# Second weight of the second MoE: plain blocks in DRAM and a split in place in the steps that load it, with new order keys for that MoE

## The chip, the cores and the metric

The kernel runs on one core of one Trainium2 chip. The metric is the time of one execution in microseconds of device time; the time of a kernel is the median of its runs. One execution is also recorded by the hardware profiler, and the rows below come from that one.

## The reference, cut to what matters

Three stages follow one another in fp32: a packed attention (4 batches, 8 heads, 576 positions), a first feed-forward block with `h * cos(h)` as its activation, and a second one with four experts whose outputs are weighted and summed. The change lies in the last stage alone:

```
N, D, E, F = 2304, 512, 4, 1024
p = domain_probs / (domain_probs.sum(-1, keepdims=True) + 1e-09)
out = zeros(N, D)
for e in range(E):
    h = maximum(x @ w1[e], 0.0)
    out += p[:, e:e + 1] * (h @ w2[e])
```

`w2` is the second weight that the title speaks of.

## The kernel before, in words

**Arithmetic.** TensorE multiplies fp32r operands. Each operand is kept as two tiles, a high part and a low part (the value minus its high part), and `mm3` (line 197) makes three matmuls for one product: high by high (L199), high by low (L200), low by high (L201). Making the two parts is called a split: ScalarE copies the value into the high part (L661), and GpSimd or VectorE subtracts that from the value (L652, the helper `split`).

**Steps of the second MoE.** The 2304 tokens are worked in three thirds (`NH` = 3), and the experts' 4 times 1024 hidden columns in eight slices of 512 (`NU` = 8). One third by one slice is a step, 24 in all, numbered n = 0 to 23. A step has a front, `b_pair` (L901), called twice (j = 0, 1): seven products of a Strassen-like scheme (`PRODUCTS`, L648), each of six matmuls of 384 columns, so 84 in a step. Their sums are made on VectorE (`add`, L931), with one copy on ScalarE for each call (L993). The back of a step stands in the order one step later:

- In the first third (steps 0 to 7) it is `b_back` (L1024): six token tiles, twelve matmuls each of 512 columns, with the four plain row blocks of w2 (tiles `w2`, keys 0 to 3) as moving operand. It ends in L1051 on VectorE.
- In the other two thirds (steps 8 to 23) it is `b_back2` (L1073), again seven products, 84 matmuls of 384 columns. They use the four plain blocks and four sums of w2's quarters, called w1 to w4 there. Its order is `BACK` (L1067): a11, w4, a12, w1, w3, w2, a22. Each ends in L1108 on VectorE. Before it, the gated activations are summed (L960) and split (`g_op`, L965), seven for each call.

**Weights.** In steps 0 to 7 `weights` (L696) loads raw blocks of w1 and w2 (`raw`, four buffers), makes the sums on VectorE (L729, `sums`), and splits seven operands of the front (tag `aop`, eight buffers) and eight of the back (tag `w2`, eight buffers: four blocks, four sums). Although `b_back` reads only the four blocks, the four sums are split too, and all fifteen split tiles, 512 KB each, are written to DRAM by `to_dram` (L670). In steps 8 to 23 `kept_weights` (L677) loads those fifteen tiles, already split, 512 KB each. The back's loads come in the order 0, 1, 2, 3, w1, w3, w2, w4 into a ring of eight buffers, so that each waits until the same buffer's last reader of the step before is done, and none is issued ahead of the one in front of it in the ring. `tokens_kept` (L805) and `kept_tokens` (L869) do for the token operands of the second and third thirds what these two do for the weights; `shares` (L886) loads, every second step, the experts' weights per token.

**Order of the work.** All instructions are put in order by a planner, class `Plan` (L27), before the program is built. Each piece of work has an engine, an assumed duration, what it waits for, the buffers that it takes, and a key. The planner takes whatever can start soonest; among pieces that can start at the same time the lower key goes first. Pieces on engines other than TensorE and the queue of SyncE (SP) take the lowest key of those who wait for them. Work of GpSimd and VectorE work on SBUF alone are never planned at the same time (`port`). A split that has `alt` may go to VectorE. A transfer is planned to occupy SP for its megabytes times `MB2` and to land 2.2 us later; `MB2` is 1/0.4 before. Every engine then runs its list in that order.

The keys of the second MoE's steps are written by hand: step n starts at k0 = 100 times its number, and `PLACE` (L1290) adds offsets:

```
PLACE = ((0, 5, 15, 20, 30, 35, 40), (10, 25, 45), (15, 30, 45, 60, 72, 84, 96))
```

The first tuple is for the seven products of `b_pair` (plus 50 for j = 1), the second for `b_back` and the third for `b_back2`, whose seven offsets belong to `BACK` in its order.

## Time and profile before

| what | value |
|---|---|
| median of 3 runs | 1175.41 us (1173.87 to 1177.24) |
| the profiled execution, its own time | 1176.87 us |
| span of its records, first to last instruction | 1175.1 us |
| TensorE busy | 1106.1 us, 94% of the span |
| VectorE, ScalarE, GpSimd busy | 832.7, 460.0, 453.4 us |
| moved by DMA | 296.23 MB, mean 252 GB/s |

The second MoE begins at about 396 us of the span. A busy TensorE row counts matmuls that overlap one another, so idle time shows only where a matmul waited long; the time between the starts of two matmuls is the better measure of pace.

### The profile page before, as it was taken

To read this page: it belongs to the slowest core of one execution; us is meant where nothing else is said; L and a number is where in the kernel's file an instruction comes from. 1 tells how busy PE (TensorE), PEld (TensorE's weight loads), DVE (VectorE), ACT (ScalarE), POOL (GpSimd) and SP (SyncE) were. 2 spreads that over 40 slices of the span, in tenths; PEclk is the share of its full clock that TensorE was granted. 3 is DMA by queue.
4 is the path that set the end of the run, shared out by engine and by line. 5 is a ranking of instruction groups with operands and counts; after the bars stand their busy time and mean duration, and the time that the engine had idled before them with its cause. 6 is when DMAs were issued, how large, how long until landed. Compare 5 with 4: busy or idle time off the path is not lost.

```text
span 1175.1 us, 19040 instructions
## 1 busy us (share of the span) xinstructions
PE 1106.1 (94%) x7241; PEld 1037.8 (88%) x7241; DVE 832.7 (71%) x1315; ACT 460.0 (39%) x788; POOL 453.4 (39%) x342
## 2 busy tenths in 40 slices
PE   7599999999999989998999999999999999999997
PEld 4478999999999978887878899999999999999997
DVE  3798777865456766678686576777777767767776
ACT  3677655554444434444344233222222232222221
POOL 1454665562224664564554133222222232222220
PEclk7799999999999999999999999999999999999999
DMA  9682433421244797998998998777777997767753
GB/s 312 225 273 95 158 117 148 149 81 41 82 143 147 271 355 281 386 387 334 406 374 324 378 373 304 269 266 270 269 256 287 391 322 262 256 239 267 250 212 125
DMA packets 101646, 296.23 MB, mean 252 GB/s; under 512 B 11500, under 2 KB 32052, under 8 KB 99508
## 3 DMA queue, kind: packets, MB, share of 16 engines
q1 hardware_dynamic: 101556, 295.02, 69.1%
q8 instruction: 57, 0.93, 0.3%
q14 instruction: 33, 0.27, 0.1%
HBM read 206.87 MB, written 88.12 MB: 251 GB/s over the span
## 4 chain that ended last, share of the span: by engine, by line
PE 73%; DMA 11%; DVE 7%; ACT 3%; issue 2%; POOL 2%; SPq 1%; DVEq 0%; ACTq 0%; POOLq 0%
PE pa L199 24%; PE pa L201 23%; PE pa L200 23%; PE pa L347 2%; DMA raw<-w 2%; DMA w<-q0w 1%; DMA w<-q3w 1%; DMA w<-q5w 1%; DVE aop L652 1%; POOL w2s L652 1%; DVE s L729 1%; DMA kt<-kT 1%; DMA w<-q1w 1%; DVE p L931 1%; DMA w<-q6w 1%
## 5 line engine op out<-in xcount | busy, mean ns | idle before, releaser
L199 PE MATMUL pa<-g,w 128*128 128x288 f32 (+1 forms) x960 | 304.8, 317 | 17.3 <-DMA w<-q3w 4.9
L200 PE MATMUL pa<-g,w 128*128 128x288 f32 (+1 forms) x960 | 302.3, 315 | 1.1 <-POOL g L584 1.1
L201 PE MATMUL pa<-g,w 128*128 128x288 f32 (+1 forms) x960 | 302.2, 315 | 0.5 <-POOL w L291 0.5
L652 POOL TENSOR_TENSOR g<-u,g 128x384 fp32r<-128x384 f32 x127 | 132.3, 1056 | 347.3 <-ACT g L661 329.8
L199 PE MATMUL pa<-bop,aop 128*128 128x384 f32 x672 | 229.6, 342 | 17.9 <-DVE p L931 7.6
L201 PE MATMUL pa<-bop,aop 128*128 128x384 f32 x672 | 228.7, 340 | 3.9 <-DVE aop L652 3.1
L200 PE MATMUL pa<-bop,aop 128*128 128x384 f32 x672 | 227.5, 338 | 0.0
L199 PEld LDWEIGHTS pa<-g,w 128*128 128x128 f32 x960 | 180.4, 188 | 24.8 <-issue 10.1
L200 PEld LDWEIGHTS pa<-g,w 128*128 128x128 f32 x960 | 180.5, 188 | 1.8 <-POOL g L584 1.8
L201 PEld LDWEIGHTS pa<-g,w 128*128 128x128 f32 x960 | 180.8, 188 | 1.0 <-POOL w L291 1.0
L661 ACT ACTIVATE g<-u 128x384 fp32r<-128x384 f32 x192 | 98.7, 523 | 191.5 <-DVE u L960 117.8
L199 PEld LDWEIGHTS pa<-bop,aop 128*128 128x128 f32 x672 | 127.5, 190 | 25.5 <-ACT w L661 7.4
L584 POOL TENSOR_TENSOR g<-t,g 128x576 fp32r<-128x576 f32 x64 | 95.2, 1500 | 119.1 <-ACT g L581 113.9
L201 PEld LDWEIGHTS pa<-bop,aop 128*128 128x128 f32 x672 | 127.2, 189 | 5.8 <-DVE aop L652 4.7
L200 PEld LDWEIGHTS pa<-bop,aop 128*128 128x128 f32 x672 | 127.5, 190 | 1.4
L931 DVE TENSOR_TENSOR p<-pa,p 128x384 f32<-128x384 f32 x144 | 79.8, 555 | 45.0 <-PE pa L201 38.8
L1108 DVE TENSOR_TENSOR acc<-pa,acc 128x768 f32<-128x768 f32 x88 | 83.9, 954 | 24.5 <-PE pa L201 24.4
L199 PE MATMUL pa<-at,m 128*128 128x288 f32 x256 | 78.3, 306 | 4.8 <-DVE t L577 3.6
L200 PE MATMUL pa<-at,m 128*128 128x288 f32 x256 | 77.1, 301 | 2.6 <-POOL at L652 2.6
L201 PE MATMUL pa<-at,m 128*128 128x288 f32 x256 | 76.8, 300 | 0.0
L199 PE MATMUL pa<-w,g 128*128 128x512 f32 x192 | 75.2, 392 | 0.0
L201 PE MATMUL pa<-w,g 128*128 128x512 f32 x192 | 75.2, 391 | 0.0
(128 smaller groups left out, 1744.6 us busy)
## 6 DMA issues: line engine op xcount, KB each, us to landing
w<-p SPq DMA_DIRECT2D x64, 512.0 KB, 5.2
at<-at SPq DMA_DIRECT2D x16, 1152.0 KB, 5.3
raw<-w SPq DMA_DIRECT2D x32, 512.0 KB, 6.3
p<-w SPq DMA_DIRECT2D x32, 512.0 KB, 5.9
raw<-w_in SPq DMA_DIRECT2D x6, 1024.0 KB, 5.2
raw<-w_out SPq DMA_DIRECT2D x6, 1024.0 KB, 7.1
vt<-vk SPq DMA_DIRECT2D x8, 576.0 KB, 7.2
kt<-kT SPq DMA_DIRECT2D x8, 576.0 KB, 9.1
```

The costliest lines, as they stand in the source:

```text
L199: nc.tensor.matmul(o, lhsT=l(0), rhs=r(0), start=first, stop=False, skip_group_check=True)
L200: nc.tensor.matmul(o, lhsT=l(0), rhs=r(1), start=False, stop=False, skip_group_check=True)
L201: nc.tensor.matmul(o, lhsT=l(1), rhs=r(0), start=False, stop=last, skip_group_check=True)
L347: nc.tensor.matmul(o(e)[32 * q:32 * q + 32, :N], lhsT=l[64 * e:64 * e + 64, 32 * q:32 * q + 32], rhs=r(q // 2, q % 2)[64 * e:64 * e + 64], ...
L584: nc.gpsimd.tensor_tensor(out=s["g"][:, 1], in0=s["t"], in1=s["g"][:, 0].bitcast(F32), op=ALU.subtract)
L652: (nc.vector if on_vector else nc.gpsimd).tensor_tensor(out=dst[:, 1], in0=src, in1=dst[:, 0].bitcast(F32), op=ALU.subtract)
L661: nc.scalar.activation(r["t"][:, 0], src(), AF.Copy)
L729: nc.vector.tensor_tensor(out=t, in0=src(a, m)(), in1=src(b, m)(), op=o)
L931: nc.vector.tensor_tensor(out=s[o] if o in s else tmp(o), in0=s[x], in1=s[y], op=ALU.add)
L1108: nc.vector.tensor_tensor(out=ac["t"], in0=ac["t"] if how == ALU.subtract else p, in1=p if how == ALU.subtract else ac["t"], op=how)
```

## The change

It does five things.

1. In the first third the four sums of w2 (w1 to w4) are no longer split. The sums themselves go to DRAM as plain fp32, 256 KB each.
2. The four plain blocks of w2 are still split for `b_back`, but what goes to DRAM is the raw block, 256 KB, straight from the tile that was loaded, and not the split pair.
3. In steps 8 to 23 each of the eight w2 tiles is loaded as 256 KB into the low half of its split tile; then ScalarE copies it to the high half, and GpSimd (or VectorE) subtracts in place.
4. The keys of the second MoE come from tables: `first` for n = 0, `one` for steps 1 to 7, `two` for 8 to 22, `end` for 23, `last` for the final back, with entries for stores (`keep`), gated splits (`g`) and the two calls of `tokens_kept` (`kept`, 150 before in both).
5. The planner's figure `MB2` goes from 1/0.4 to 1/0.37.

```diff
-    MB2 = 1 / 0.4
+    MB2 = 1 / 0.37
...
+    def plain(u, x, src, shape, ready, slot, at):
+        def f():
+            w2_d[u, x] = dpool.tile(shape, F32, tag=f"w{u}{x}", name=f"w{u}{x}", bufs=1)
+            nc.sync.dma_start(out=w2_d[u, x], in_=src())
+
+        return dma(0.26 * MB2, f, [ready], [], [slot], at)
...
+        def split_in_place(x, shape, src, after):
+            W[x] = r = {"slot": pl.slot("w2")}
+            at = 100 * len(its) + 100 * n + 50
+
+            def f():
+                r["t"] = bp["w2"].tile(shape, F32R, tag="w2", name="w2", bufs=8)
+                load(r["t"][:, 1].bitcast(F32), src())
+
+            def f_hi():
+                nc.scalar.activation(r["t"][:, 0], r["t"][:, 1].bitcast(F32), AF.Copy)
+
+            def f_lo(v=False):
+                split(r["t"], r["t"][:, 1].bitcast(F32), v)
+
+            a = dma(0.26 * MB2, f, after, [r["slot"]])
+            a = pl.op("ACT", 0.63, f_hi, [a], [], [r["slot"]])
+            r["ready"] = pl.op("POOL", 1.3, f_lo, [a], [], [r["slot"]], alt=0.7)
+
...
-        for x in (0, 1, 2, 3, "w1", "w3", "w2", "w4"):
-            kept(x, "w2", w2_d, [P, 2, 512] if x in range(4) else [P, 2, 2, 256])
+        for k in range(4):
+            split_in_place(k, [P, 2, 512], lambda k=k: w2_d[u, k], [w2_d["op", u, k]])
+        for x in ("w1", "w3", "w2", "w4"):
+            split_in_place(x, [P, 2, 2, 256], lambda x=x: w2_d[u, x], [w2_d["op", u, x]])
...
-        keep = 100 * len(its) + 100 * n + 60
+        keep = 100 * len(its) + 100 * n + KEYS["keep"][0]
...
-            w2_d["op", u, k] = to_dram(w2_d, (u, k), [P, 2, 512], f"p{u}{k}", lambda k=k: W[k]["t"], W[k], keep + 30)
-        sums(2, keep + 40)
+            w2_d["op", u, k] = plain(u, k, lambda k=k: raw[2, k // 2][:, k % 2], [P, 512], ld[2, k // 2], sr[2, k // 2], keep + KEYS["keep"][1])
+        sums(2, keep + KEYS["keep"][2])
         for i in range(1, 5):
-            x = f"w{i}"
-            W[x] = hi_lo("w2", lambda: bp["w2"].tile([P, 2, 2, 256], F32R, tag="w2", name="w2s", bufs=8), src(f"s{i}", 2),
-                         (0.63, 1.3, 0.61), need(2, f"s{i}"), uses(2, f"s{i}"), 3, keep + 50)
-            w2_d["op", u, x] = to_dram(w2_d, (u, x), [P, 2, 2, 256], f"q{u}{x}", lambda x=x: W[x]["t"], W[x], keep + 60)
+            w2_d["op", u, f"w{i}"] = plain(u, f"w{i}", src(f"s{i}", 2), [P, 2, 256], S[2, f"s{i}"]["op"], S[2, f"s{i}"]["slot"],
+                                           keep + KEYS["keep"][3])
...
+        gkey = keys[6] + KEYS["g"][j]
...
-            gkey = k[6] + 40
...
+            'end': {'a': [7.7, -4.1, 13.5, 9.7, 25.5, 36.8, 44.1, 51.4, 31.1, 65.2, 55.6, 83.4, 100, 147.1],
+                    'b': [7.6, 30, 37.1, 56.9, 58.3, 96.2, 118.8]},
...
+            'first': {'a': [-2.9, -27.5, 4.6, 13.1, 46.9, -9.5, 50.4, 5, 11.5, 37, 54.3, 58.5, 40.6, 95.8]},
+            'g': [38.7, 40.8],
...
+            'keep': [100.6, -134.8, 1.6, 6.3],
+            'kept': [169.3, 260.8],
+            'last': {'b': [18.3, 53.6, 64, 91.6, 70.2, 69.5, 211.3]},
...
+            'one': {'a': [27.2, 17, 18.9, 77, 37, 81.6, 28.9, 33.7, 63.9, 48.4, 67, 78.4, 79.5, 60.1],
+                    'b': [25.1, 36, 39.1, 80, 56, 81.7]},
+            'out0': [-122.9, -853.4],
+            'two': {'a': [-6.8, 28.5, 26, 19.7, 29.1, 43.6, 40, 7.4, 46.4, 66, 71.1, 67.6, 82, 91.3],
+                    'b': [15, 25.5, 40.7, 56.3, 70.6, 84.4, 93.8]}}
...
-    PLACE = ((0, 5, 15, 20, 30, 35, 40), (10, 25, 45), (15, 30, 45, 60, 72, 84, 96))
...
+        place = KEYS["first"] if n == 0 else KEYS["one"] if h == 0 else KEYS["end"] if n >= NSTEP - 1 else KEYS["two"]
         if n > NU:
-            b_back2(n - 1, Ws.pop(n - 1), [k0 + x for x in PLACE[2]])
+            b_back2(n - 1, Ws.pop(n - 1), [k0 + x for x in KEYS["last" if n == NSTEP else "two" if n < NSTEP - 1 else "end"]["b"]])
...
-            tokens_kept((n + 1) // 2, k0 + 150)
+            tokens_kept((n + 1) // 2, k0 + KEYS["kept"][n // 2])
```

## Rows read from the trace of the kernel before

**Rows 1.** Page, parts 1 and 2: TensorE's busy time; DMA's busy tenths in 40 slices.
```profile
PE 1106.1 (94%) x7241; PEld 1037.8 (88%) x7241; DVE 832.7 (71%) x1315; ACT 460.0 (39%) x788; POOL 453.4 (39%) x342
...
DMA  9682433421244797998998998777777997767753
```
**Rows 2.** Busy time by stretch; its first line names the columns.
```profile
core 0: us, PE busy (x) PEld busy (x) DVE busy (x) ACT busy (x) POOL busy (x), PEclk, DMA share, GB/s
...
411.80:657.40 245.60, 226.53 (x1095) 199.04 (x1094) 178.70 (x277) 101.88 (x192) 121.77 (x83) 0.99 0.94 358
657.40:1123.50 466.10, 448.16 (x2510) 440.28 (x2509) 340.97 (x570) 127.24 (x247) 126.90 (x122) 1.00 0.80 290
813.50:842.90 29.40, 29.40 (x170) 29.40 (x169) 23.49 (x40) 8.12 (x16) 8.31 (x8) 1.00 0.74 260
...
1123.50:1175.10 51.60, 44.37 (x253) 43.72 (x251) 37.43 (x58) 10.19 (x20) 10.32 (x10) 0.98 0.40 142
```
**Rows 3.** Timeline of TensorE in a back of the first third: start, duration.
```profile
545.17 0.39 PE L200 MATMUL pa<-w,g 128*128 128x512 f32 x1
545.40 0.39 PE L201 MATMUL pa<-w,g 128*128 128x512 f32 x1
```
**Rows 4.** What TensorE waited for, 396 to 657.4 us: total, times, longest.
```profile
PE pa L199 <- DVE p L931: 7.1, 5, 2.5
PE pa L199 <- ACT w L661: 4.4, 3, 2.0
PE pa L201 <- DVE aop L652: 3.1, 5, 1.1
PE pa L199 <- ACT g L980: 2.7, 3, 0.9
PE pa L199 <- ACT p L993: 1.0, 1, 1.0
PE pa L199 <- DVE g L983: 0.8, 1, 0.8
PE pa L201 <- POOL aop L652: 0.7, 1, 0.7
```
**Rows 5.** What TensorE waited for, 657.4 to 1123.5 us.
```profile
PE pa L199 <- DMA w<-q3w: 4.9, 2, 2.5
...
PE pa L199 <- DVE g L652: 4.1, 3, 2.3
...
PE pa L199 <- DMA w<-q4w: 0.5, 1, 0.5
```
**Rows 6.** Timelines of SP's queue and TensorE around the wait at 787 us.
```profile
779.98 0.99 SPq L191 DMA_DIRECT2D w<-q3w  x2
...
789.32 0.41 PE L199 MATMUL pa<-g,w 128*128 128x384 f32 x1 [2.54 <-DMA w<-q3w]
```
**Rows 7.** ScalarE's and GpSimd's groups, 411.8 to 657.4: busy, mean ns, idle before.
```profile
L661 ACT ACTIVATE w<-raw 128x512 fp32r<-128x512 f32 x28 | 17.0, 622 | 20.9 <-DMA q4w<-w2s 5.2 <-DMA q3w<-w2s 5.0 <-DMA q2w<-w2s 3.2
...
L652 POOL TENSOR_TENSOR w2s<-s,w2s 128x512 fp32r<-128x512 f32 x27 | 39.2, 1478 | 68.8 <-ACT w2s L661 68.8
```
**Rows 8.** Transfers by kind: issues, KB each, median us from issue to landing.
```profile
w<-p SPq DMA_DIRECT2D x64, 512.0 KB, 5.2
...
ptile<-pT SPq DMA_DIRECT2D x1, 256.0 KB, 2.9
```
**Rows 9.** VectorE's and ScalarE's groups, 657.4 to 1123.5 us.
```profile
L960 DVE TENSOR_TENSOR u<-u 128x384 f32<-128x384 f32 x58 | 33.5, 578 | 0.9
...
L652 DVE TENSOR_TENSOR g<-p,g 128x384 fp32r<-128x384 f32 x25 | 14.4, 578 | 4.3 <-ACT g L661 2.8
...
L993 ACT ACTIVATE p<-pa 128x384 f32<-128x384 f32 x30 | 14.8, 492 | 74.0 <-PE pa L201 74.0
```
**Rows 10.** Splits of the sums of w2, 411.8 to 657.4: ns min/median/max.
```profile
L652 POOL TENSOR_TENSOR w2s<-s,w2s x27: 1262/1305/2010, 412.3 to 656.0; 128x512 fp32r<-128x512 f32 x27
...
L652 DVE TENSOR_TENSOR w2s<-s,w2s x3: 681/682/844, 452.3 to 657.2; 128x512 fp32r<-128x512 f32 x3
```

## The prediction made before the change was run

> **What bounds the kernel now.** I read the page first: TensorE is busy for 94% of the span, and the DMA engines are nearly full in the middle slices [rows 1]. So TensorE sets the time, and what can be won is where it falls behind its own pace. Then the busy times by stretch. The stretch 813.5 to 842.9 is step 13, with 168 matmuls and no gap: 29.40 us, or 0.175 a matmul of 384 columns [rows 2]. That is the pace of a step in the last two thirds. Matmuls of 512 columns start 0.23 us apart [rows 3], so a step of the first third has a pace of 84 times 0.175 (14.7) plus 72 times 0.23 (16.6), 31.3 us.
>
> Against these paces the rows of stretches say what is lost. Steps 1 to 7 run from 411.8 to 657.4: 245.6 us against 7 times 31.3 (219.1), 26.5 lost. Steps 8 to 22 run from 657.4 to 1123.5: 466.1 against 15 times 29.40 (441.0), 25.1 lost. The end, from 1123.5, holds 252 matmuls, 44.1 of its 51.6 us, and the rest is mostly the sums and stores behind the last product [rows 2]. In the first third the DMA engines are 94% busy; in steps 8 to 22, 80%.
>
> Then the waits, each stretch by itself. Up to 657.4 TensorE waits 19.8 us in seven rows, on VectorE's sums, on splits of front operands, and on ScalarE where that copies plain blocks of w2 [rows 4]. What stands behind the last is seen in ScalarE's idle time: in front of the 28 copies `w<-raw` it idles 20.9 us, 13.4 of them until stores of split sums have landed (`q4w<-w2s` and its like), because a w2 buffer is free only when its store is done [rows 7]. In the last two thirds six rows name loads of split sums, from `q3w` down to `q4w`, 13.0 us together; the splits of gated sums come next with 4.1 [rows 5]. One such wait in full: two loads of `q3w` are issued at 780.0 to 781.0, TensorE is ready at 786.8 and goes on at 789.3 [rows 6]. The block is w4, second in the back's order, last in the ring: about 6.8 us of room, and a load that takes 8 to 9.
>
> **The change, part by part.**
>
> *First third, transfers.* Each step writes eight tiles of 256 KB instead of 512: 2.1 MB less, 14.7 MB in seven steps. The stretch moves 358 GB/s for 245.6 us, 87.9 MB [rows 2]; 73.2 are left, which at the same rate and share would take 204 us, under the 219 of TensorE's pace. DMA stops being the bound there, with little to spare.
>
> *First third, engines.* Four copies on ScalarE (0.62 us each) and four subtractions (1.48 on GpSimd) go from each step, some 5.9 us of GpSimd's 17.4 [rows 2, 7]. The w2 ring holds two steps' blocks, and no block's buffer waits for a store. So ScalarE's 13.4 us before `w<-raw` go. Of TensorE's 26.5 I take away the three rows of waits on ScalarE (8.1), half of the four on VectorE and GpSimd (5.9 of 11.7), and 2 of the 6.7 that no row names [rows 4]: 16 us, and 10.5 stay (1.5 a step), since the products' sums on VectorE are as many as before. Bounds: nothing, or all 26.5; a loss too, since the store of a sum now holds one of four `s` buffers for the next step's sums: at most the whole 7.1 of the first row of waits once more [rows 4].
>
> *Moved stores and tokens.* The stores of front tiles get a later key (from 60 to 100.6), the blocks an earlier one; the second `tokens_kept` moves from 150 to 260.8. Keys decide only among transfers that could start together, bytes stay the same, and the tokens are needed ten steps later: nothing, covered by the room that the first part makes on the queue. Without that room they would hold the front's buffers, as the seven rows of waits show now.
>
> *Last two thirds, transfers.* Eight loads of a step halve. The trace has no load of 256 KB under load: from below the one of `ptile`, 2.9 us to landing, from above the median of `w<-p`, 512 KB, 5.2 [rows 8]. I take 4, the middle, since the other loads of a step still share the queue. Behind it w4 now needs a copy (0.62) and a subtraction (1.48 at most on GpSimd, 0.68 on VectorE) [rows 7, 10]: 6.1 us in all against 6.8 of room. So the 13.0 us of waits on loads fall to some 3, for steps in which a split has to queue: 10 us won. Bounds: with 8.7 as now and 2.1 behind it every w4 would be late by 4, a loss of 15 times 4 less the 13 of now, 47 us; from above a gain of 13, and up to 25.1 if the new order covers the gated splits too.
>
> *Last two thirds, engines.* ScalarE takes 8 times 0.62 more, 13.2 us of a step's 29.4. VectorE's 341 us in 15 steps are 22.7 a step, GpSimd's 8.5 [rows 2]. Whether GpSimd can take eight more at 1.48 (11.8) hangs on VectorE's work on SBUF alone: five groups from `u<-u` down to `g<-p,g`, 127.8 us, 8.5 a step [rows 9]. 8.5 and 8.5 and 11.8 are 28.8 of 29.4 if the two never overlap. Some splits on VectorE at 0.68 relieve that. It fits, narrowly: priced at nothing, covered by the engines' idle time, with the rest in the rivals.
>
> *Order and the planner's figure.* `MB2` moves no byte; it makes the plan count 1.4 instead of 1.3 us for 512 KB. The trace cannot price a new order. It cannot win more than is lost, counted above; I take nothing and 8 us either way for the range. The same for the end (51.6 against 44.1).
>
> *Sum.* The profiled execution took 1176.87 us, 1.8 more than its span, 1.46 over the median of the runs. 1176.9 less 16 less 10 is 1150.9; less 1.5 for the median, 1149.
>
> **Weighed against the Trainium skill.** The trace moves 358 GB/s with transfers of mostly 512 KB, many in flight [rows 2, 8]. The page SBUF — State Buffer, section The DMA setup-cost knee, says that each transfer pays about 2 us whatever its size, and gives 2 us plus bytes over 436 GB/s. By that, as an estimate, halving a block saves 0.6 us, not half: w4 would be as late as now. The sum would lose its second term, which is rival B; the rate above speaks against a price paid one by one, but not against one paid by each landing. The same page, section Who interferes with whom, calls the access that VectorE and GpSimd share an exclusive lock, taken by a VectorE instruction with two SBUF inputs against a GpSimd one that reads SBUF. The trace agrees in kind: the same split took 1262 to 2010 ns on GpSimd [rows 10]. That is rival E.
>
> **The rivals.**
>
> *B: the split eats what the smaller load gives back.* What a block waits for is queue and latency, its landing stays at 5.2 to 8.7 us, and copy and subtraction come on top. For it: w4's place in the ring is not changed. Against it: a new order can leave more room. The last two thirds keep their 466.1 us: 1176.9 less 16 less 1.5, 1159.
>
> *C: the first third keeps its loss.* Its waits name VectorE and splits, not transfers; five sixths of the bytes are left. Only the 4.4 us on ScalarE go, and some 2 of the unnamed: 1176.9 less 6.4 less 10 less 1.5, 1159.
>
> *D, slower: loads that land later than planned block ScalarE.* Now a late load holds only the product that reads it. Afterwards the copy of a block stands in ScalarE's list where the planner expects the landing, 0.26/0.37 and 2.2, 2.9 us after issue. If it lands at 5.2, whatever is behind it waits 2.3: among that the copies L993, thirty in 15 steps [rows 9], on which VectorE's sums and the next products hang. Less one product of slack (6 times 0.175), 1.25 each and two a step make 37 us. With 16 won in the first third and the 13 of waits on loads gone, 1176.9 plus 8 less 1.5: 1183. It decides from 1 us a copy on, that is, landings 2.0 us late at each. Against it: thirty copies stand among 120 such landings, and ScalarE idles over half of a step.
>
> *E: GpSimd and VectorE together become the bound.* Were each split stretched to the 2.01 us of the worst one, 8.5 and 8.5 and 16.1 are 33.1 us a step, 2.0 over now, 31 in 15 steps: with the first third's gain 1190. It costs from 1.55 us a split on, and makes the whole slower from 1.9.
>
> *F: order given back.* The gains go into waits that the new order makes: 1175.
>
> **How the numbers follow.** My forecast has 0.48, B 0.18, C 0.13, D 0.11, E 0.04, F 0.06. A difference under 0.3% (3.5 us) is about what a measurement of this kernel cannot tell from no change. Faster is the forecast with B and C: 0.79; same F: 0.06; slower D and E: 0.15. The forecast's own range is 1139 to 1158 (8 us for the order, some for the terms). The range reaches from 1136 to 1174: it leaves out D, E, half of F, and the low edge of the forecast.
>
> **What would show it.** In the changed kernel steps 1 to 7 should take some 230 us and DMA be busy for under 0.9 of them; no copy of a plain block waits for a store. Steps 8 to 22 should take some 456, with DMA under 0.65, ScalarE near 13 and GpSimd 15 to 20 us a step, and few waits of TensorE that name splits of w2. I am wrong if TensorE waits for copies or sums behind blocked ScalarE (D), if splits on GpSimd last over 1.55 on average (E), or if the back's second product waits as now, on a split (B).

## The result and the profile after

The changed kernel takes 1159.22 us, median of 4 runs (1154.72 to 1159.94), against 1175.64 us of the kernel before in the same comparison. The ratio is 0.9853 with an interval of [0.9824, 0.9881]: faster by 16.4 us. The forecast was 1149 in a range from 1136 to 1174. The sign and the range held; of the 26.4 us that were forecast, 16.4 came.

The busy times by stretch say where. The keys are new, so steps are cut at the same events in both kernels: the first product of step 0, of step 8 and of step 22, and the end. First the kernel before, cut this way; the columns are those of [rows 2].

```profile
396.00:657.40 261.40, 241.36 (x1179) 213.56 (x1178) 186.32 (x290) 111.36 (x209) 131.82 (x89) 0.99 0.92 351
657.40:1091.80 434.40, 418.44 (x2341) 410.85 (x2340) 317.41 (x531) 119.12 (x231) 118.61 (x114) 1.00 0.80 291
1091.80:1175.10 83.30, 74.09 (x422) 73.16 (x420) 60.99 (x97) 18.31 (x36) 18.61 (x18) 0.99 0.53 190
```

The same of the changed kernel:

```profile
394.80:638.30 243.50, 237.54 (x1178) 212.54 (x1178) 181.14 (x277) 94.06 (x178) 112.18 (x76) 0.99 0.89 323
638.30:1065.30 427.00, 416.21 (x2330) 406.40 (x2330) 319.89 (x500) 170.72 (x333) 278.60 (x237) 1.00 0.66 219
1065.30:1157.10 91.80, 79.32 (x433) 77.61 (x431) 68.57 (x101) 31.13 (x63) 53.40 (x46) 0.95 0.37 118
1076.60:1080.00 3.40, 3.36 (x10) 3.36 (x11) 1.67 (x3) 1.81 (x5) 3.40 (x4) 0.50 0.00 0
...
1084.00:1090.00 6.00, 6.00 (x37) 6.00 (x36) 3.97 (x6) 2.23 (x5) 2.60 (x3) 1.00 0.63 206
```

The first third falls from 261.4 to 243.5 us, by 17.9. Steps 8 to 21 fall from 434.4 to 427.0, by 7.4, although DMA is busy for 0.66 instead of 0.80. Steps 22 and 23 with the end grow from 83.3 to 91.8, by 8.5. With 1.2 us before step 0 that makes the 18.0 us between the two spans. The cut at step 22 does not divide quite the same work: the new order puts one product of a back, 12 matmuls or 2.1 us at 0.175, behind it (2330 and 433 matmuls against 2341 and 422). Some 2 us of the 7.4 and of the 8.5 have thus only changed sides. From step 8 to the end both stretches together went from 517.7 to 518.8 us: the whole gain is in the first third. GpSimd is the engine whose time changed most: 118.6 to 278.6 us in steps 8 to 21, with ScalarE going from 119 to 171. (The last two lines belong to the last section.)

What TensorE waits for in steps 8 to 21 of the changed kernel:

```profile
PE pa L199 <- DVE u L975: 6.0, 8, 2.3
PE pa L199 <- DVE p L958: 3.7, 5, 2.3
PE pa L201 <- POOL w L652: 0.7, 1, 0.7
```

No load of w2 is in the list, where six rows with 13.0 us stood [rows 5]. In their place stand VectorE's gated values (L975, before L948) and the products' sums (L958, before L931). From 1065.3 on, in the same view:

```profile
PE pa L199 <- DVE p L958: 3.8, 1, 3.8
PE pa L200 <- DVE g L652: 1.6, 1, 1.6
PE pa L201 <- DVE w L652: 1.0, 1, 1.0
```

In the first third, ScalarE's idle time in front of the copies of plain blocks, 20.9 us in [rows 7], is zero in the changed kernel's groups (second line below). The halved loads of plain blocks land after a median of 2.8 us (first line, from the page's list of transfers), sooner than either bound that the prediction had, 2.9 and 5.2 [rows 8]. Those of the sums, w4 among them, take longer: by slice their medians in steps 8 to 21 are 2.9 to 3.6 us. All halved loads together have 2.5, 3.1 and 11.0 us as shortest, median and longest.

```profile
w<-w SPq DMA_DIRECT2D x64, 256.0 KB, 2.8
```

```profile
L661 ACT ACTIVATE w<-raw 128x512 fp32r<-128x512 f32 x32 | 18.2, 623 | 0.0
```

**Where the time of steps 8 to 21 went.** One view shows it: the instructions of one tile, with the shortest, the median and the longest duration in ns. Before, tiles `g` and `u`, which VectorE makes from two inputs in SBUF:

```profile
L652 DVE TENSOR_TENSOR g<-u,g x55: 545/558/560, 679.0 to 1090.7; 128x384 fp32r<-128x384 f32 x55
L960 DVE TENSOR_TENSOR u<-p,u x54: 546/552/941, 682.3 to 1078.6; 128x384 f32<-128x384 f32 x54
```

After:

```profile
L652 DVE TENSOR_TENSOR g<-u,g x50: 546/556/1650, 652.1 to 1051.1; 128x384 fp32r<-128x384 f32 x50
L987 DVE TENSOR_TENSOR u<-p,u x52: 546/552/1653, 660.5 to 1048.2; 128x384 f32<-128x384 f32 x52
L975 DVE SCALAR_TENSOR_TENSOR u<-pa,share x82: 542/557/559, 648.1 to 1058.2; 128x384 f32<-128x384 f32 x82
```

Minimum and median are as before, but the longest take 1.65 us, as if 1.1 us, about one GpSimd split, had been put in front. The third line is the check: the same engine and nearly the same time, but one input in PSUM, and not one of 82 is stretched, although 63 of them run while GpSimd works. The mean of `u<-p,u` went from 561 to 786 ns, of `g<-u,g` from 556 to 840.

One such pair from the timelines of GpSimd and VectorE:

```profile
683.84 1.61 POOL L652 TENSOR_TENSOR w<-w 128x512 fp32r<-128x512 f32 x1
684.22 1.65 DVE L652 TENSOR_TENSOR g<-u,g 128x384 fp32r<-128x384 f32 x1
```

GpSimd's split ends at 685.45, VectorE's at 685.87. It is the same each time: of the 157 gated sums and splits on VectorE in these steps (`u<-p,u`, `u<-u`, `g<-u,g`, `g<-p,g`), 44 take over 0.7 us, and every one of them ends 0.41 to 0.42 us after a GpSimd split that overlaps it, 31 times a split of w2 and 13 times a gated one. Together they take 29.8 us longer than their usual 0.555. Before, it was 5 of 186 with 2.3 us. So VectorE waits for the end of GpSimd's instruction and then does its work.

### The profile page after: what moved, and what is told of

The parts are those of the page before. It is cut to its first block, busy times and chain, and to the rows that moved or that the text cites. A ratio compares the mean times of both kernels' runs of the same rounds, so it can differ in the third digit from the quotient of the medians.

```text
span 1157.1 us, 19197 instructions
## 1 busy us (share of the span) xinstructions
PE 1103.4 (95%) x7241; PEld 1036.0 (90%) x7241; DVE 833.9 (72%) x1270; ACT 507.1 (44%) x884; POOL 630.0 (54%) x483
## 4 chain that ended last, share of the span: by engine, by line
PE 77%; DVE 13%; DMA 4%; ACT 2%; issue 2%; POOL 1%; SPq 1%; DVEq 0%; ACTq 0%; POOLq 0%
PE pa L199 26%; PE pa L201 25%; PE pa L200 25%; PE pa L347 2%; DVE p L958 1%; DVE u L987 1%; DVE g L652 1%; DVE pa L958 1%; DMA w<-w7w 1%; DVE g L1010 1%; DMA w<-w 1%; DVE acc L1134 1%; DVE u L975 1%; DMA kt<-kT 1%; DMA w6w<-s 1%
## 5 line engine op out<-in xcount | busy, mean ns | idle before, releaser
L652 POOL TENSOR_TENSOR w<-w 128x512 fp32r<-128x512 f32 x122 | 164.4, 1359 | 102.7 <-ACT w L706 97.9
L652 POOL TENSOR_TENSOR g<-u,g 128x384 fp32r<-128x384 f32 x132 | 139.0, 1065 | 80.6 <-ACT g L661 80.6
L661 ACT ACTIVATE g<-u 128x384 fp32r<-128x384 f32 x192 | 95.5, 518 | 138.1 <-DVE u L987 112.2
L706 ACT ACTIVATE w<-w 128x512 fp32r<-128x512 f32 x128 | 79.6, 628 | 115.7 <-DMA w<-w 64.4
L958 DVE TENSOR_TENSOR p<-pa,p 128x384 f32<-128x384 f32 x144 | 79.4, 554 | 57.5 <-PE pa L201 53.8
```

The costliest lines, as they stand in the source:

```text
L652: (nc.vector if on_vector else nc.gpsimd).tensor_tensor(out=dst[:, 1], in0=src, in1=dst[:, 0].bitcast(F32), op=ALU.subtract)
L661: nc.scalar.activation(r["t"][:, 0], src(), AF.Copy)
L706: nc.scalar.activation(r["t"][:, 0], r["t"][:, 1].bitcast(F32), AF.Copy)
L958: nc.vector.tensor_tensor(out=s[o] if o in s else tmp(o), in0=s[x], in1=s[y], op=ALU.add)
```

## The experiments

Two theories stood against each other. **P**: the in-place subtractions on GpSimd block VectorE's two-input instructions, by an access to SBUF that both need, so the halved loads are paid for by VectorE's stretched work. **L**: loads land later than planned, and the copies that wait for them block ScalarE's list (rival D). Beside them the question of what the order alone does (**O**). Times of stretches below come from the profiled execution of each kernel; ratios are against the kernel before on the same chip.

### The two halves of the change alone

The data path with the old order:

```diff
-    MB2 = 1 / 0.37
+    MB2 = 1 / 0.4
...
-            'g': [38.7, 40.8],
+            'g': [40, 40],
...
-            'keep': [100.6, -134.8, 1.6, 6.3],
-            'kept': [169.3, 260.8],
+            'keep': [60, 30, 40, 60],
+            'kept': [150, 150],
...
+    for x in ("one", "two", "end"):
+        KEYS[x] = {"a": [50 * j + y for j in range(2) for y in (0, 5, 15, 20, 30, 35, 40)],
+                   "b": [15, 30, 45, 60, 72, 84, 96]}
+    KEYS["one"]["b"] = [50 * j + y for j in range(2) for y in (10, 25, 45)]
+    KEYS["first"]["a"] = [14 * i + 7 * j for j in range(2) for i in range(7)]
+    KEYS["last"]["b"] = KEYS["two"]["b"]
```

> The changed kernel's data path (plain blocks and sums in DRAM, split in place) with the order of before: PLACE's offsets, 40 for the gated splits, 60/30/40/60 for the stores, 150 for the tokens, 1/0.4 for the planner. Theory P (port): in the last two thirds what the halved loads win is given back because splits of w2 on GpSimd and VectorE's work on SBUF block each other, whatever the order. Then the first third keeps most of its 18 us gain and the last two thirds stay near 465 us: 1156 to 1164. Theory O (order): the new keys make or lose the time. If they carry the gain, this kernel is near before's 1175; if they cost the second gain, it is near 1149.

Measured: 1165.29 us, ratio 0.9900 [0.9861, 0.9939]. Its runs spread from 1156.89 to 1171.12; the profiled one was the fastest of them. First third 244.5, steps 8 to 21 426.6, end 89.6. The median lies 1.3 us above what P expected and near neither of the two values of O. Its interval overlaps that of the changed kernel (0.9824 to 0.9881), so on the new data path the order alone made little difference.

And the new order with the old data path:

```diff
-        for k in range(4):
-            split_in_place(k, [P, 2, 512], lambda k=k: w2_d[u, k], [w2_d["op", u, k]])
-        for x in ("w1", "w3", "w2", "w4"):
-            split_in_place(x, [P, 2, 2, 256], lambda x=x: w2_d[u, x], [w2_d["op", u, x]])
+        for x in (0, 1, 2, 3, "w1", "w3", "w2", "w4"):
+            kept(x, "w2", w2_d, [P, 2, 512] if x in range(4) else [P, 2, 2, 256])
...
-            w2_d["op", u, k] = plain(u, k, lambda k=k: raw[2, k // 2][:, k % 2], [P, 512], ld[2, k // 2], sr[2, k // 2], keep + KEYS["keep"][1])
+            w2_d["op", u, k] = to_dram(w2_d, (u, k), [P, 2, 512], f"p{u}{k}", lambda k=k: W[k]["t"], W[k], keep + KEYS["keep"][1])
...
-            w2_d["op", u, f"w{i}"] = plain(u, f"w{i}", src(f"s{i}", 2), [P, 2, 256], S[2, f"s{i}"]["op"], S[2, f"s{i}"]["slot"],
-                                           keep + KEYS["keep"][3])
+            x = f"w{i}"
+            W[x] = hi_lo("w2", lambda: bp["w2"].tile([P, 2, 2, 256], F32R, tag="w2", name="w2s", bufs=8), src(f"s{i}", 2),
+                         (0.63, 1.3, 0.61), need(2, f"s{i}"), uses(2, f"s{i}"), 3, keep + KEYS["keep"][3])
+            w2_d["op", u, x] = to_dram(w2_d, (u, x), [P, 2, 2, 256], f"q{u}{x}", lambda x=x: W[x]["t"], W[x], keep + KEYS["keep"][3] + 1)
```

> The other half alone: the new order keys and 1/0.37, with before's data path (fifteen tiles of 512 KB stored and loaded, sums split in the first third, nothing split in place). Theory P and the prediction's first term (bytes and splits removed free the first third): the first third stays near before's 261 us from its first product on, DMA at 0.94 of it; the last two thirds lose their waits on loads only as far as the order alone can, 455 to 466; in all 1165 to 1180. Theory O: near the changed kernel's 1159.

Measured: 1187.28 us, ratio 1.0086 [1.0053, 1.0119]: slower than before, and slower than either theory expected. Its stretches, then what TensorE waited for in the first third, and last the one row of its waits from step 8 to 21:

```profile
396.70:678.70 282.00, 244.91 (x1178) 216.41 (x1177) 213.09 (x322) 109.99 (x205) 91.19 (x61) 0.93 0.87 325
678.70:1102.90 424.20, 417.13 (x2330) 408.34 (x2329) 324.25 (x549) 116.84 (x232) 100.96 (x96) 1.00 0.82 298
1102.90:1185.50 82.60, 76.25 (x434) 75.21 (x432) 63.88 (x99) 18.34 (x36) 20.21 (x19) 0.99 0.55 197
```

```profile
PE pa L199 <- DVE oacc L1077: 21.5, 2, 21.2
PE pa L201 <- DVE aop L652: 7.5, 1, 7.5
```

```profile
PE pa L199 <- DVE u L975: 7.1, 14, 3.6
```

The one wait of 21.2 us ends at 597.7. On VectorE's timeline the sum behind it (L1077) stands after a token subtraction that waited 8.4 us for its load, and after token splits:

```profile
592.98 0.96 DVE L854 TENSOR_TENSOR ys<-ys 128x768 f32<-128x768 f32 x1 [8.40 <-DMA ys<-y]
594.04 2.92 DVE L868 TENSOR_TENSOR ys<-ys 128x768 fp32r<-128x768 f32 x3
596.88 0.74 DVE L1077 SCALAR_TENSOR_TENSOR oacc<-pa,pr,oacc 128x512 f32<-128x512 f32 x1
```

So with the old data path the moved token work does cost (DMA's share is 0.94 from 576 to 598), and the new data path is what makes the new order usable in the first third. But the other two stretches read the other way: with old data the same keys give 424.2 and 82.6 us, less than the 434.4 and 83.3 of before. And TensorE no longer waits for any load of w2 there, although the loads have 512 KB and land no sooner (plain blocks 6.5 us, 5.2 before). The order by itself was worth 10.9 us from step 8 on; in the changed kernel, which has the same order and the same cuts, the data path cost 2.8 and 9.2 us more than that.

### The cost that was suspected, taken away

Plan, order, loads and copies stay; the in-place subtraction is made on an eighth of its columns. The kernel leaves out the rest, so its output is not the reference's.

```diff
-                split(r["t"], r["t"][:, 1].bitcast(F32), v)
+                c = (slice(None), slice(0, 64)) if len(shape) == 3 else (slice(None), slice(None), slice(0, 32))
+                (nc.vector if v else nc.gpsimd).tensor_tensor(
+                    out=r["t"][:, 1][c], in0=r["t"][:, 1][c].bitcast(F32), in1=r["t"][:, 0][c].bitcast(F32), op=ALU.subtract)
```

> The changed kernel with its plan and its order untouched, but each in-place subtraction of w2 in steps 8 to 23 works on an eighth of the columns; the rest of the subtraction is left out. Loads, copies on ScalarE, waits and order are the same. Theory P: GpSimd holds the shared access for 11 us less a step, VectorE's stretched sums and splits (776, 843 and 644 ns on average) go back to some 560, and the 13.5 us that TensorE waits for VectorE go: steps 8 to 22 fall from 465 to 450-455, in all 1143 to 1149. Theory L (loads land late and block ScalarE's list): the loads and copies are unchanged, so the time stays at 1156 to 1161.

Measured: 1146.47 us, ratio 0.9731 [0.9699, 0.9764], far outside the changed kernel's interval. The stretches from step 8 on, and VectorE's two groups there (busy, mean ns, idle before):

```profile
639.80:1058.30 418.50, 414.78 (x2330) 406.68 (x2329) 296.17 (x500) 171.54 (x335) 172.14 (x239) 1.00 0.67 223
1058.30:1147.30 89.00, 78.19 (x433) 76.55 (x431) 61.90 (x101) 29.71 (x60) 33.74 (x45) 0.97 0.38 124
```

```profile
L652 DVE TENSOR_TENSOR g<-u,g 128x384 fp32r<-128x384 f32 x50 | 31.3, 645 | 2.7 <-ACT g L661 2.4
L990 DVE TENSOR_TENSOR u<-p,u 128x384 f32<-128x384 f32 x52 | 28.1, 567 | 0.0
```

Steps 8 to 21 take 418.5 instead of 427.0 us, with the sums back at 567 ns, the splits at 645, 14 of 157 stretched instead of 44, and TensorE's waits at 3.3 us in place of 10.4. Time and means are what P expected; L's 1156 to 1161 is out. One thing changes with the blocking: GpSimd's list is 106 us shorter (172.1 for 278.6), so what waits for GpSimd comes sooner too. In the changed kernel that path is short: one wait of TensorE of 0.7 us names GpSimd, and none of VectorE's groups waits for it. The end falls by 2.8 only: its larger loss is not P.

### Half of it, and another engine for it

Storing the four plain blocks split, as before, leaves only four in-place splits a step:

```diff
-            split_in_place(k, [P, 2, 512], lambda k=k: w2_d[u, k], [w2_d["op", u, k]])
+            kept(k, "w2", w2_d, [P, 2, 512])
...
-            w2_d["op", u, k] = plain(u, k, lambda k=k: raw[2, k // 2][:, k % 2], [P, 512], ld[2, k // 2], sr[2, k // 2], keep + KEYS["keep"][1])
+            w2_d["op", u, k] = to_dram(w2_d, (u, k), [P, 2, 512], f"p{u}{k}", lambda k=k: W[k]["t"], W[k], keep + KEYS["keep"][1])
```

> Between the two kernels: the four plain blocks go to DRAM split, 512 KB each, as before; only the four sums are stored plain and split in place. The keys are the changed kernel's. Theory P: half of the new GpSimd work is gone, so about half of the stretch; steps 8 to 22 fall by 4 to 8 us, while the first third gives back 2 to 6 for 1 MB more in each step: in all 1153 to 1159. Theory L: half of the late copies are gone too, a similar size, but the stretched durations on VectorE would stay as they are. If DMA were still the bound, it is slower: 1162 to 1168.

Measured: 1164.34 us, ratio 0.9876 [0.9845, 0.9908]. First third 250.3, steps 8 to 21 429.0, end 87.9. The first third paid 7, steps 8 to 21 gave nothing, and steps 8 to 22 fell by 3.3 where 4 to 8 were expected: a miss. The blocking was halved: 24 of 166 gated sums and splits on VectorE are stretched (over 0.7 us), by 14.3 us together instead of 29.8, and the mean of `g<-u,g` fell to 605 ns. TensorE's waits stayed at 11.1 us (10.4 in the changed kernel) under other names, on VectorE, ScalarE and the sums of the output. Half of the blocking was thus not half of the time, and why is not shown; this kernel is also planned anew and gets another order from the same keys.

The subtraction on VectorE alone:

```diff
-            r["ready"] = pl.op("POOL", 1.3, f_lo, [a], [], [r["slot"]], alt=0.7)
+            r["ready"] = pl.op("DVE", 0.7, lambda: f_lo(True), [a], [], [r["slot"]], port=True)
```

> The changed kernel with the in-place subtraction on VectorE alone (0.7 us planned), none on GpSimd; order planned anew from the same keys. Theory P: GpSimd then holds the shared access no longer than before the change, so the stretch of VectorE's work on SBUF goes back to the 560-580 ns of before; but VectorE has 22.7 and 5.6, 28.3 us of work in a step of 29.4, and there is no room for a late input. Steps 8 to 22: 455 to 470, in all 1150 to 1165. Theory L: copies behind late loads hold VectorE now instead of GpSimd: 470 to 485.

One run: 1159.18 us, beside 1179.92 of before. Steps 8 to 21 take 432.4, the end 86.1. The sums `u<-p,u` are down to a mean of 630 ns, where P expected 560 to 580, and 14 of 129 are stretched, all behind gated splits; but VectorE is now busy for 357 of the 432 us (320 of 427 in the changed kernel), its sums come late for that, and the stretch is longer, not shorter. L's 470 to 485 for steps 8 to 22 is out: 464.7.

### The first third's bytes

Each plain store is made twice, the second into a place that nothing reads: the bytes written are those of before, the engines' work and order those of after.

```diff
             nc.sync.dma_start(out=w2_d[u, x], in_=src())
+            d2 = dpool.tile(shape, F32, tag=f"v{u}{x}", name=f"v{u}{x}", bufs=1)
+            nc.sync.dma_start(out=d2, in_=src())
```

> The changed kernel with each of the first third's eight plain stores made twice, the second into a place that nothing reads: the bytes of before (DMA near 0.95 in the first third), the engines' work, waits and keys of the changed kernel. Theory B (the bytes freed the first third, the prediction's first term): from the first product to step 8 it grows from 243.5 by 10 to 18 us, to 254-261, in all 1168 to 1178. Theory S (the splits and buffers that were removed freed it): 244 to 249 us, in all 1158 to 1165.

Measured: 1171.44 us, ratio 0.9936 [0.9908, 0.9964]. In its profile the first third is back at 260.4 us, with DMA at 0.98:

```profile
395.90:656.30 260.40, 243.00 (x1177) 214.54 (x1177) 183.55 (x276) 93.98 (x177) 113.21 (x77) 0.98 0.98 363
```

So the first third's gain is the bytes: with them back, the removed splits by themselves leave 260.4 us against the 261.4 of before. A second store also holds the tile that it reads until it has landed, and no run takes that apart from the bytes. The profiled execution was one of the slower ones of its ten (1166.3 to 1175.9); by the medians the bytes are worth some 10 us, by this profile 17.

### The end

The old order gave 89.6 us for the end and the new one 91.8, which holds 12 matmuls (2.1 us) more, so the two are alike; with old data the new order gave 82.6. The loss sits in the data path. Two kernels ask where. First the old offsets for steps 8 to 22 only:

```diff
+    KEYS["two"] = {"a": [50 * j + y for j in range(2) for y in (0, 5, 15, 20, 30, 35, 40)],
+                   "b": [15, 30, 45, 60, 72, 84, 96]}
```

> The changed kernel with PLACE's offsets for steps 8 to 22 only; the first third, the end and the last back keep the new keys. In the kernel with all of the old order, steps 8 to 22 took 456 us in its profile and the end 59.8. If the new keys of these steps cost time on their own: 1146 to 1152. If that profile was one good execution (its runs spread over 14 us) and the blocking strikes either order: 1156 to 1163.

Measured: 1156.83 us, ratio 0.9820 [0.9763, 0.9877]; steps 8 to 21 429.2, end 88.5. The interval covers the changed kernel's ratio, and the time is what was expected if the blocking strikes either order. The traces bear that out: 46 of 151 gated sums and splits are stretched here by 29.9 us, and 38 of 149 by 25.0 in the kernel with all of the old order.

Then slices 6 and 7 treated as before, so that steps 14, 15, 22 and 23 load split tiles for the slices that they bring in:

```diff
+            if u >= 6:
+                kept(k, "w2", w2_d, [P, 2, 512])
+                continue
             split_in_place(k, [P, 2, 512], lambda k=k: w2_d[u, k], [w2_d["op", u, k]])
...
+            if u >= 6:
+                x = f"w{i}"
...
+                w2_d["op", u, x] = to_dram(w2_d, (u, x), [P, 2, 2, 256], f"q{u}{x}", lambda x=x: W[x]["t"], W[x],
+                                           keep + KEYS["keep"][3])
+                continue
```

> The changed kernel, but slices 6 and 7 of every third are treated as before: split in the first third, stored and loaded as 512 KB. So steps 14, 15, 22 and 23 have no in-place split. DMA is busy for a quarter of the end only, so the bytes should be free there. Theory P: steps 22 and 23 fall from 91.9 to 84-87 us, the first third loses 1 to 3: in all 1151 to 1157. If the end's loss is a matter of its new order: 1158 to 1163.

Measured: 1152.92 us, ratio 0.9790 [0.9733, 0.9848]; the interval overlaps that of the changed kernel. The end is 87.0, the first third 242.7. What is left of the end's loss is in step 22, whose back is that of step 21, slice 5. In the changed kernel the stop there reads like this, from the timelines of SP, ScalarE, VectorE and TensorE:

```profile
1064.56 0.33 SPq L191 DMA_DIRECT2D w<-w5w  x1
...
1071.24 0.63 ACT L706 ACTIVATE w<-w 128x512 fp32r<-128x512 f32 x1 [4.21 <-DMA w<-w5w]
1071.78 0.92 ACT L661 ACTIVATE g<-u 128x384 fp32r<-128x384 f32 x2
...
1072.32 1.79 DVE L652 TENSOR_TENSOR g<-u,g 128x384 fp32r<-128x384 f32 x2 [1.68 <-ACT g L661]
1074.04 2.08 DVE L987 TENSOR_TENSOR u<-u 128x384 f32<-128x384 f32 x2
1076.04 1.80 DVE L958 TENSOR_TENSOR p<-pa,p 128x384 f32<-128x384 f32 x3
...
1076.64 0.69 PE L199 MATMUL pa<-bop,aop 128*128 128x384 f32 x1 [3.83 <-DVE p L958]
```

A load issued at 1064.56 lands 6.6 us later, where loads of its kind have a median of 3.1; it stands on the queue behind two loads of 512 KB and two of `shares`, and why it was late was not tried. ScalarE stands before its copy for 4.21 us; behind the copy in its list are the copies of two gated splits; behind those, on VectorE, the splits and two sums stretched to 1.0 us each; and behind them the sum for which TensorE stops for 3.83 us. That is L and P in one chain. The test was slice 5 kept split too:

```diff
-            if u >= 6:
+            if u >= 5:
```

> As the kernel in which slices 6 and 7 keep the old data path, with slice 5 too, so that step 22, in which the changed kernel's longest stop lies (TensorE waits 3.8 us behind a load of slice 5's sum, a copy, a gated split and two sums), has no in-place split at all. Theory L for the end (a late load blocks ScalarE's list there): steps 22 and 23 fall from 87.0 to 82-84 us; the first third pays 1 to 2 for 2 MB more; in all 1148 to 1152. Theory P alone: that stop was stretched VectorE work, most of it gone already; 86 to 88, in all 1152 to 1156.

Measured: 1163.01 us, ratio 0.9894 [0.9857, 0.9931], where 1148 to 1152 were expected; 82.5 us for the end: L's number, and no wait of TensorE over 0.3 us is left there. But the first third came to 256.6, with a stop of 9.3 us in step 6, where the splits and stores of slice 5 now meet the token work and a late raw load. So the end's loss goes when no load there has a copy and a split behind it; the kernel as a whole was no faster than the changed one.

### A version that keeps both

Slices that were split in place in the second third are written back split, and the last third loads them so; the first third is left alone.

```diff
             r["ready"] = pl.op("POOL", 1.3, f_lo, [a], [], [r["slot"]], alt=0.7)
+            if u >= 5:
+                again[0]["op", u, x] = to_dram(again[0], (u, x), shape,
+                                               f"z{u}{x}", lambda x=x: r["t"], r, 100 * len(its) + 100 * n + 200)
...
+        if n >= 2 * NU and u >= 5:
+            for x in (0, 1, 2, 3, "w1", "w3", "w2", "w4"):
+                kept(x, "w2", again[0], [P, 2, 512] if x in range(4) else [P, 2, 2, 256])
+            return W
```

> The changed kernel, with its first third untouched; in the second third the tiles of slices 5, 6 and 7 that were split in place are also written to DRAM, 512 KB each, and the last third loads them split. So steps 22 and 23 have no in-place split, at the price of 4.2 MB more in each of steps 13 to 15, where DMA has room (0.65 busy). If the end's loss is late loads and in-place splits in steps 22 and 23, as the kernel with three slices kept split in the first third showed (82.5 us), and that kernel's first-third stop came from its extra work there: first third 243-245, steps 8 to 21 425-429, steps 22 and 23 82-84, in all 1147 to 1152. If any extra byte brings its stop along: 1155 to 1165.

> The same for slices 3 to 7, so that half of the last third has no in-place split and five steps of the second third write 4.2 MB more. Theory P: steps 20 and 21 lose their blocking too, 1 to 2 us on the kernel with slices 5 to 7: 1146 to 1151; if the stores hold w2 buffers so that loads come late: 1152 to 1160.

> The same for all eight slices: every step of the second third writes its split tiles (8 times 512 KB), and the last third has no in-place split at all. Theory P: steps 17 to 21 lose what blocking is left, 1 to 3 us on the kernel with slices 3 to 7; the second third moves some 10 MB in a step of 30 us, near the rate at which DMA bound the first third before. If that is still under the bound: 1144 to 1149; if it is the bound: 1152 to 1165.

With slices 5 to 7: 1155.81 us, ratio 0.9811 [0.9785, 0.9837]. First third 242.5 and end 82.6, near what was expected; but steps 8 to 21 took 433.4 in the profile, with a new stop of 4.7 us in step 20, and the time is in the range named for that case. With slices 3 to 7: 1148.43 us, ratio 0.9753 [0.9724, 0.9782], the fastest of the kernels that do all of the work, and clear of the changed kernel's interval. Its stretches:

```profile
396.00:641.60 245.60, 237.72 (x1177) 212.41 (x1177) 183.00 (x276) 93.89 (x177) 111.96 (x77) 0.99 0.89 321
641.60:1066.20 424.60, 416.47 (x2330) 406.38 (x2329) 325.00 (x505) 162.97 (x319) 259.24 (x224) 1.00 0.80 282
1066.20:1148.90 82.70, 76.33 (x434) 75.14 (x432) 63.93 (x99) 18.34 (x36) 20.24 (x19) 0.99 0.57 195
```

Its gain is in the end, 82.7 for 91.8, and not in less blocking: 41 of 161 of VectorE's gated sums and splits are still stretched in steps 8 to 21, by 29.0 us.

With all eight slices: 1152.26 us, ratio 0.9778 [0.9735, 0.9821], steps 8 to 21 428.2 with DMA at 0.89. The second third is then near the load at which the first third suffered (0.92), and more slices did not make it faster; the two intervals overlap. Why five slices avoid the stop in step 20 that three have was not tried.

## Why the prediction was right or wrong, point by point

The prediction cut the time at the first products of steps 1, 8 and 23, where both kernels have done the same number of matmuls. Step 0 before, and then the four stretches of the changed kernel:

```profile
396.00:411.80 15.80, 14.84 (x86) 14.52 (x85) 7.63 (x14) 9.49 (x17) 10.05 (x7) 1.00 0.70 238
```

```profile
394.80:415.10 20.30, 17.26 (x85) 15.95 (x85) 16.23 (x23) 8.86 (x17) 9.86 (x6) 0.92 0.84 290
415.10:638.30 223.20, 220.28 (x1094) 196.59 (x1094) 164.92 (x255) 85.21 (x161) 102.32 (x70) 1.00 0.90 326
638.30:1103.40 465.10, 450.48 (x2509) 440.29 (x2509) 348.63 (x543) 184.25 (x360) 302.90 (x258) 0.99 0.65 215
1103.40:1157.10 53.70, 45.05 (x254) 43.72 (x252) 39.84 (x59) 17.60 (x36) 29.09 (x25) 0.97 0.24 79
```

The sum was 16 and 10 and 0. What came is 22.4 in steps 1 to 7, 1.0 in steps 8 to 22 and minus 2.1 in the end, with minus 4.5 in step 0 and 1.2 ahead of it, for which the prediction had no term. The range held by its allowance for the order and by a first term that came out larger than its size; the second term failed.

**The first third: right in mechanism, undersized.** 16 us were forecast for steps 1 to 7, 22.4 came, and step 0 gave 4.5 of them back; with the old order on the new data it takes 15.2. Of the prediction's causes the bytes are shown by the stores made twice, which bring 260.4 us and DMA at 0.98 back; the removed splits by themselves are worth about 1 us in that profile. ScalarE's wait for w2 buffers went to zero as written.

**Moved stores and tokens: right for this data path, the condition not settled.** Priced at nothing if the queue has room. With the old data path the same keys made waits of 21.2 and 7.5 us. But the full queue alone does not make them: with the stores made twice the same keys run at a DMA share of 0.98, and the longest wait is 2.8. Which part of the old data path it takes, the bytes, the splits or the buffers that its stores hold, is not shown.

**Loads of the last two thirds: the waits went, the time did not.** A gain of 10 of the 13 us of waits was forecast. All of these waits went, but the halved loads were not needed for it: with the new order and old data none is left either, with loads that land as late as before. The prediction gave the order nothing, and there it was worth 10.9 us. From step 8 to the end the profiles have 517.7 us before, 506.8 with the order alone, 516.2 with the data path alone, 518.8 with both, and 507.5 with both and an eighth of the subtraction. So what the halved loads won beyond the order cannot be told from nothing in these profiles, and the subtraction took back what the order had given.

**Engines of the last two thirds: the step that failed.** The prediction counted 28.8 of 29.4 us for GpSimd and VectorE's work on SBUF together, wrote "it fits, narrowly", and priced it at nothing. A shared access that is 98% booked by count is not free: measured, 465.1 against 453.2 us in steps 8 to 22 when seven eighths of the subtraction are taken away, 11.9 us, of which 8.5 are in steps 8 to 21. The text of rival E looked for it in the wrong place, in splits on GpSimd that get longer. These took 1.36 us on average, under E's 1.55; the ones that cost time were VectorE's, and they stand in front of the sums for TensorE. (ScalarE's 13.2 us a step are 13.4 by the row and the term beside them; nothing hangs on it.)

The Trainium skill, page SBUF — State Buffer, section Who interferes with whom, says that a VectorE instruction with two SBUF inputs contends with a GpSimd instruction that reads SBUF, that one with at most one SBUF input does not outside certain faster modes, and that whichever issues second is blocked fully. The trace agrees: up to 1.65 us for what takes 0.55, each time until 0.41 to 0.42 us after GpSimd's end, and none of 82 stretched when one input is in PSUM.

**Steps 22 and 23: a late load, rival D at one place.** The prediction's end, from step 23 on, lost 2.1 us and stays within its 8. The stop of 3.83 us lies in step 22. Against the old data in the same order, steps 22 and 23 with the end lost 9.2 us (91.8 and 82.6): 2.8 of that goes with the subtraction (89.0), and without in-place splits there the stretch takes 82.5 to 83.4. The chain shown is D's mechanism, a late load in front of ScalarE's list, but not in front of the copies L993, as D had it: the copies of the gated splits stand behind it.

**The rivals.** B's time, 1159, is the time measured, and its 466.1 us for steps 8 to 22 is nearly the 465.1 that came, but B is not what happened: B let loads land as late as before, and they landed in about half the time (plain blocks 2.8 us for 5.2). That its number fits is luck. C fell with the first third, F and the slower outcomes with the time. Of the signs, DMA's share (0.90 and 0.65), ScalarE (12.3 us a step), GpSimd (20.2) and the few waits of TensorE on splits of w2 (0.7 us in all) came within a little of what was written; steps 8 to 22 took 465 and not 456.

The Trainium skill, page SBUF — State Buffer, section The DMA setup-cost knee, would by the prediction's estimate have a block save 0.6 us by being halved. No run here takes size apart from traffic: the plain blocks went from 5.2 to 2.8 us while DMA's share fell from 0.80 to 0.66. Within one kernel, that with slices 6 and 7 split as before, the plain blocks have medians of 4.4 us with 512 KB and 2.8 with 256, in different steps; in the one that loads slices 5 to 7 back split it is 3.7 and 4.1, the other way round.

## What to carry to other kernels

When a change moves work from transfers to engines, add up not only each engine's time but what two engines share: here VectorE was busy for 75% of steps 8 to 21 and GpSimd for 65%, and they still blocked one another, and the one that got longer stood in front of TensorE. In a list that an engine runs in order, put work behind a load where the load's worst landing is covered, not its usual one; near the end of this program, where DMA's share is 0.37, it was cheaper to load the finished form. And judge an order and a data path apart: the same keys lost 20.6 us in the first third with the old data and won 10.9 in the other two, and a gain that is put down to smaller loads may be one that the order gives alone.

## What the runs showed of the hardware that was not expected

After the stop of 3.83 us the granted clock in the stretch 1076.6 to 1080.0 is 0.50, that is 1.2 GHz: the line stands with the stretches above. From 1070 to 1076, most of which is the stop, the mean was 0.97, and 1084 to 1090 is at 1.00 again. Matmuls of 384 columns start 0.32 us apart just behind the stop instead of 0.175, so this stop cost more than its own time. The same kernel on one core also spread more than the 0.3% that was assumed: the data path in the old order from 1156.9 to 1171.1 us in six runs, the kernel before from 1171.4 to 1182.5 in the ten beside it. Single profiles of these kernels therefore say where time goes better than how much.
